# Three big buffers laid out in pairs, with the first transposes split and a new order of work

## The chip, the cores and the metric

The kernel runs on one core of a Trainium2 chip. The metric is the device time of the whole launch in microseconds; three runs of the kernel before gave 157.53 to 160.98, with a median of 159.81.

## The reference

An input `x` of 2048 positions by 512 channels goes through two branches and is mixed by a gate:

```python
g = _sigmoid((x * gate_w).sum(-1, keepdims=True))
a = irfft2(rfft2(x) * (w_r + 1j * w_i), s=(S, D))      # spectral filter over positions and channels
# b: a long convolution over positions, channel by channel:
A = -exp(log_A_real) + 1j * A_imag
C = (C_real + 1j * C_imag) * exp(log_dt)[:, None]
K = 2.0 * einsum("dn,dnl->dl", C, exp((A * dt[:, None])[:, :, None] * pos)).real
b = irfft(rfft(u, 2L) * rfft(K, 2L), 2L)[:, :L] + u * D_skip
return g * a + (1 - g) * b
```

All data are float32.

## The kernel before, in words

All data stay in SBUF, 128 partitions wide. Branch b is a running sum of each channel along the positions when the exponents are small enough; the kernel tests that and otherwise takes a general path, which the inputs of these runs do not take. Branch a is the two-dimensional transform, done as products on TensorE (PE).

The work is cut into steps of one letter and one digit. `PLAN`, a string, lists them, and a loop issues each step's instructions in that order; each engine and each DMA queue then runs its own instructions in the order in which they were issued, waiting for data and for buffers. PSUM is a pool of four buffers of two banks each (tag `ps`), used in rotation. The steps are:

- **C, c**: first half of the transform over the positions. `C` (PE) multiplies a part of the input, lying in `AI`, into a PSUM tile `p_s`; for three parts POOL makes sums and differences `f` first (`F`). `c` (DVE, L259) is one transpose in blocks of 32 by 32 from `p_s` into the buffer `AR`. There are nine parts, seven of 128x1024 and two of 128x512.
- **P, t**: `P` (PE, L372) takes 128 columns of `AR` as the weights, multiplies by a table `s2e` into `p_t`; `t` (ACT, L377) copies out to `et`. There are nine units of this and the following steps; unit 0 is half as large. A product of float32 data appears as two matmul instructions, each with its weight load (PEld).
- **D, d, Z, W, U**: the channel transform (PE, `p_d`, L388), a copy (ACT, L392), sums in PSUM (DVE, L398 to L401) and the multiplication by the filter `w` (DVE, L412 to L416). SP's queue brings `w` for each unit (`l`), and a small row of it (`L`, L363).
- **p, g, h**: sums on POOL (L423, L424 and L435, L436) into `px` and `gt`, and one corrected row (ACT, L442, L443).
- **I, i, V**: the inverse channel transform (PE, `p_v`, L454, weights from `gt`), a copy (ACT, L459), and sums (DVE, L467), which write the buffer `AI`. `K` corrects slot 0 of it.
- **B, b**: inverse transform over the positions, first half, when all units are done: `B` (PE, L486) reads `AI`, four 64x64 tiles of the array at a time, into `p_ia`; `b` (DVE, L489) transposes into `VA`, which is the memory of `AR` under another view. There are eight.
- **Q**: second half (PE, L521): 128x256 of `VA` times a table `s1a` into `p_oa`. `q` (DVE, L542) scales by the gate and adds in one go; `a` (ACT, L532) and `A` (POOL, L536) do the same in two steps. Both end in the stores. There are eight.
- **X, x, y, m, n, r, o, Y, s**: branch b. Load of a 1 MB piece of `XT` (SP, L292), two scalings (ACT, L296 and L300), a running sum (DVE, L304), the even positions (POOL, L308), a DMA that adds the result into `XT` (POOL, L314), the skip term (ACT, L311), transposes of `XT` (PE, `p_y`, L497) and their scaling by one minus the gate into `bs` (ACT, L509).
- **R**: loads of tables; `G`, `J`, `N`: gate, corrections of the filter's edge rows, and the test of the exponents.

Before the change `AR` lies as `[u, t, s]`, with 32 values of `s` together:

```python
    AR = keep.tile([P, 2, P, 32], F32, name="AR")
    VA = AR.rearrange("p u t s -> p (u t) s")
```

so that `P` reads its 128 weights, and `Q` its 256 columns, at steps of 32 floats, and `B` reads `AI` at steps of 256 floats.

Of the kernel before, what the change touches and what calls it, by code (L numbers as in the profile page):

```python
# [9 lines left out]
F32 = mybir.dt.float32  # L10
# [5 lines left out]
P = 128  # L16
# [6 lines left out]
NS = 3  # L23

PLAN = """
C0 X0 c0 C2 c2 F1 F3 C1 C4 c1 c4 C3 c3 R6 C6 N0 N1 F5 C5 c6 c5 C7 c7 R2 N3 R0 R3 C8 c8 x0 P6 y0 X1 t6 J0 R7 J1 R1 P1
l6 R4 m0 y1 x1 m1 J2 t1 D6 d6 P8 t8 P7 l1 n0 N2 l8 t7 D1 L6 d1 n1 Z6 X2 L1 U6 W6 Z1 R5 X3 P0 W1 D8 l0 p6 g6 U1 d8 h6
t0 L8 Z8 L0 G0 o1 l4 l7 W8 o0 L4 U8 D0 d0 L7 D7 d7 G1 p1 I6 l3 o2 o3 Z0 g1 U0 G2 Z7 p8 W0 P4 t4 i6 r0 g8 U7 h1 L3 D4
W7 h8 V6 d4 Z4 W4 y2 p0 U4 P3 t3 x2 I1 o4 I8 i1 x3 r1 m2 y3 i8 V1 G4 R8 g0 l5 G5 G3 L5 o5 p7 P5 h0 p4 V8 o7 n2 m3 o6
D3 d3 g7 l2 t5 P2 D5 h7 I0 Z3 t2 r2 W3 n3 r3 U3 I7 g4 d5 D2 h4 i7 Z5 p3 W5 U5 L2 p5 i0 V0 I4 V7 d2 K0 g3 Z2 i4 U2 h3  # L30
K1 g5 S0 h5 Y2 W2 p2 I3 i3 s2 g2 V4 I5 i5 Y0 V3 h2 s0 V5 Y3 I2 Y1 S1 i2 V2 B7 s3 B3 B4 b7 S3 s1 b3 B2 b4 B5 B6 B1 b2
B0 S2 b5 b6 b1 Y6 s6 Y4 b0 s4 Q6 Q4 a6 a4 Q1 a1 A6 Y7 A4 s7 Y5 Q0 Q2 q0 A1 q2 Q7 q7 s5 Q5 Q3 q5 q3
"""
UNITS = [8, 0, 1, 2, 3, 4, 5, 6, 7]
ORDER = [8, 9, 0, 1, 10, 2, 11, 3, 12, 4, 13, 5, 14, 6, 15, 7, 16]
# [123 lines left out]
def body(ctx: ExitStack, tc: tile.TileContext, x, xg, xt, w, wh, prms, vecs, gw, dskip,  # L159
         c_s1e, c_s1f, c_s2e, c_s2, c_s2v, c_s2r, c_s2q, c_s1b, c_s1a, c_dfw, c_dbw, c_pos, c_eye, out):  # L160
    nc = tc.nc
    V, G, S, T = nc.vector, nc.gpsimd, nc.scalar, nc.tensor
# [3 lines left out]
    def psum(name):  # L166
        return ps.tile([P, 2, 512], F32, tag="ps", name=name)

    keep = ctx.enter_context(tc.tile_pool(name="keep", bufs=1))
    eye = keep.tile([P, P], F32, name="eye")  # L170
    g1 = keep.tile([P, 2, 32], F32, name="g1")
    count = keep.tile([1, 1], I32, name="count")


    AR = keep.tile([P, 2, P, 32], F32, name="AR")
    VA = AR.rearrange("p u t s -> p (u t) s")

    wst = ExitStack()
    work = wst.enter_context(tc.tile_pool(name="work", bufs=1))
# [1 line left out]
    AI = work.tile([P, 17, D], F32, name="AI")  # L181
# [11 lines left out]
    s0, dsk, one, m_, nm = pers[:, 0:4], pers[:, 8:12], pers[:, 12:13], pers[:, 13:14], pers[:, 14:15]  # L193
    s2e = work.tile([P, 17, P], F32, name="s2e")
    s2v = work.tile([P, 64], F32, name="s2v")
# [12 lines left out]
    t_ = {}  # L208

    with tc.manual_schedule():  # L210
# [45 lines left out]
        def c_a(q):  # L256
            k = PARTS[q]
            n = 32 * (k.stop - k.start)
            V.transpose(AR.rearrange("p u (h t) s -> p h u (t s)", h=2)[..., 32 * k.start:32 * k.stop], t_["c", q][:, :, :2 * n].rearrange("p h (u n) -> p h u n", u=2))  # L259


        big, sm = few[:, 1:3], few[:, 3]
# [87 lines left out]
        def nrow(pr):  # L350
            return 64 if pr == 8 else P
# [14 lines left out]
        def P_(u):  # L366
            pr = UNITS[u]
            p = t_["pt", u] = psum("p_t").rearrange("p k (q c r) -> p (k q) c r", q=2, c=2)
            for v in range(nrow(pr) // 64):
                sl, k = (0, 16) if pr == 8 else (2 * pr + v, 2 * pr + v)  # L370
                for q in range(4):
                    T.matmul(p[:, q, :, 64 * v:64 * v + 64], AR[:, q % 2, :, 16 * (q // 2) + sl], s2e[:, k], start=True, stop=True)  # L372

        def t_a(u):
            n = nrow(UNITS[u])
# [86 lines left out]
        def V_(u, ks=(0, 1)):  # L462
            pr = UNITS[u]
            n = nrow(pr) // 64
            ai = AI[:, 2 * pr:2 * pr + n].rearrange("p s (h k t) -> p s h k t", h=2, k=2)
            for k in ks:
                V.tensor_tensor(ai[:, :, :, k], t_["pi", u][:, :n, :, 0], t_["po", u][:, :n], op=ALU.subtract if k else ALU.add)  # L467

# [9 lines left out]

        def B_(k):
            p = t_["pb", k] = psum("p_ia")  # L480
            av = AI.rearrange("p s (e t) -> p t (s e)", e=2)[:, 32 * k:32 * k + 32]
            for x in range(2):
                for z in range(2):
                    r = slice(64 * z, 64 * z + 64)
                    y = 16 * (z ^ x)
                    T.matmul(p[64 * x:64 * x + 64, z], s2v[r], av[r, :, y:y + 16], start=True, stop=True, tile_position=(64 * z, 64 * x))  # L486

        def b_a(k):
            V.transpose(VA[:, 32 * k:32 * k + 32].rearrange("p t (z i) -> p t z i", z=2), t_["pb", k].rearrange("p z (t i) -> p t z i", i=16))  # L489


        def Y_(j):
# [25 lines left out]
        def Q_(j):  # L518
            p = t_["pq", j] = psum("p_oa").rearrange("p k (b d) -> p (k b) d", b=2)
            for k in range(4):  # L520
                T.matmul(p[:, k], s1a[j // 2][:, 4 * j % 8 + k], VA[:, :, 4 * j + k], start=True, stop=True)  # L521

# [16 lines left out]
        def q_a(j):  # L539
# [16 lines left out]

        todo = {
            "f": lambda q: fold(q, V), "F": lambda q: fold(q, G), "C": C_, "c": c_a, "N": lambda k: N_[k](),
            "X": load_x, "x": x_a, "m": scan, "o": skip, "y": y_a, "n": lambda k: even(k, G), "k": lambda k: even(k, V), "r": both, "G": G_, "J": J_, "l": load_w, "L": load_h,
            "P": P_, "t": t_a, "D": D_, "d": d_a, "Z": Z_, "W": lambda u: W_(u, 0, V), "U": lambda u: W_(u, 1, V), "p": p_a, "g": g_a, "h": h_a, "I": I_, "i": i_a, "V": V_,  # L560
            "K": K_, "B": B_, "b": b_a, "Y": Y_, "s": s_a, "S": load_a, "Q": Q_, "q": q_a, "a": a_a, "A": A_a, "R": lambda k: loads[k](),
        }
        for word in PLAN.split():
# [5 lines left out]
    with tc.If(n_small < D):  # L569
        with tc.tile_pool(name="dram", bufs=1, space=bass.MemoryType.DRAM) as dp:  # L570
            Kd = dp.tile([D, L], F32, name="Kd")
            with tc.tile_pool(name="kg", bufs=1) as kg:
# [25 lines left out]
                for c in range(0, D, NC):  # L598
                    def tmp(name, dt=F32):
                        return kg.tile([P, NC, 96], dt, name=name, bufs=2)  # L600

                    pb = pos.rearrange("p (o l) -> p o l", o=1).broadcast_to([P, NC, 96])
# [5 lines left out]
                    for k in range(2):  # L608

                        ri, r, z = tmp("ri", I32), tmp("r"), tmp(f"z{k}")  # L610
# [23 lines left out]
                    for j in range(NC // 4):  # L634
                        for q in range(4):
                            d = NC // 4 * q + j
# [14 lines left out]
            with tc.tile_pool(name="gx", bufs=1) as gx:  # L651
                s1f = gx.tile([P, 2, P], F32, name="s1g")
                nc.sync.dma_start(s1f, c_s1f)
                for dst, isk in ((KR, True), (AG, False)):
# [4 lines left out]
                    for h in range(2):  # L659
# [6 lines left out]
                        for e in range(2):  # L666
                            for c in range(4):
                                o = 32 * c
                                p = psum("p_g1")
                                for u in range(2):  # L670
                                    q = 2 * c + u
# [6 lines left out]
            for i, pr in enumerate(ORDER):  # L678
                rows = 64 if pr == 8 else P
                slots = [2 * pr, 2 * pr + 1] if pr < 8 else ([0] if pr == 8 else [2 * pr - 2, 2 * pr - 1])  # L680
                s2 = gw2.tile([P, 2, 2, 64], F32, name="s2g", bufs=2)
# [16 lines left out]
            p = psum("p_sp")  # L698
# [3 lines left out]
            for c in range(16):  # L702
                p = psum("p_gb")
# [6 lines left out]
            for j in range(8):  # L710
# [7 lines left out]
                for i in range(4):  # L718
                    b = 4 * j + i
                    p = psum("p_go")  # L720
                    for e in range(2):
                        T.matmul(p[64 * e:64 * e + 64, 1, 0:256], gb[:, i], AG[:, b, 256 * e:256 * e + 256], start=True, stop=True)
                    T.matmul(p[:, 0, 0:256], ga[:, i], VA[:, :, b], start=True, stop=True)
                    o = ot[:, i]
# [63 lines left out]
```

## Time and profile before

The profiled execution took 160.45 us, with a span of 158.7 us of recorded work.

| engine | busy, us | share of the span | instructions |
|---|---|---|---|
| PE (matmuls) | 138.0 | 87% | 817 |
| PEld (weight loads) | 100.8 | 64% | 817 |
| DVE | 87.1 | 55% | 127 |
| ACT | 62.2 | 39% | 111 |
| POOL | 70.6 | 44% | 62 |

Weight loads overlap with matmuls. The DMA engines moved 26.56 MB, most of it in the first 40 us. The shares are means over stages with different limits, so they do not say by themselves what an engine's time is worth.

### The profile page before, as it was taken

What the parts mean: (1) busy time and instruction counts of PE and PEld (TensorE: products, weight loads), DVE (VectorE), ACT (ScalarE), POOL (GpSimd) and SP (SyncE); (2) the same over time, 40 slices, a digit from 0 to 9 for tenths busy, and PEclk for the clock granted to TensorE, in tenths of its full rate; (3) what the DMA queues carried; (4) which work ended last, traced back from release to release, by engine and by line L of the source; (5) the groups of instructions that cost most, each with busy time, mean ns of one, the idle gap of its engine ahead of it and who ended that gap; (6) DMA issues with size and microseconds to landing.
All of it is one profiled execution on the core that took longest, in us unless ns stands there. A gap on an engine that the chain in (4) does not pass through costs nothing. (4 is left out here: it accounts for less than half of the span.)

```text
span 158.7 us, 2220 instructions
## 1 busy us (share of the span) xinstructions
PE 138.0 (87%) x817; PEld 100.8 (64%) x817; DVE 87.1 (55%) x127; ACT 62.2 (39%) x111; POOL 70.6 (44%) x62
## 2 busy tenths in 40 slices
PE   7568969999999879959999898779999999999910
PEld 7435659999929758949997687624546447444400
DVE  0117985483599953899479996135664000254440
ACT  0003034813284864599444356850004646500000
POOL 0337011566669963969894999000000067400000
PEclk9999996999999956996899999999999999999995
DMA  4999999889323799723999712000000014174450
GB/s 136 292 319 415 413 393 308 320 302 382 96 82 121 214 203 220 179 52 115 255 213 178 262 28 108 0 0 0 4 0 0 0 46 180 46 266 169 169 192 16
DMA packets 9301, 26.56 MB, mean 167 GB/s; under 512 B 1697, under 2 KB 2497, under 8 KB 8257
## 3 DMA queue, kind: packets, MB, share of 16 engines
q1 hardware_dynamic: 8704, 22.13, 39.4%
q0 software_dynamic: 576, 4.19, 14.0%
q8 instruction: 8, 0.13, 0.3%
q14 instruction: 13, 0.10, 0.2%
HBM read 17.90 MB, written 4.19 MB: 139 GB/s over the span
## 5 line engine op out<-in xcount | busy, mean ns | idle before, releaser
L372 PE MATMUL p_t<-s2e,AR 128*128 128x128 f32 x136 | 31.3, 392 | 3.1 <-DVE AR L259 1.4
L372 PEld LDWEIGHTS p_t<-s2e,AR 128*128 128x128 f32 x136 | 30.6, 312 | 4.1 <-DVE AR L259 1.8
L521 PE MATMUL p_oa<-AR,s1a 128*128 128x256 f32 x64 | 28.0, 609 | 0.0
L521 PEld LDWEIGHTS p_oa<-AR,s1a 128*128 128x128 f32 x64 | 13.0, 205 | 13.6 <-issue 13.4
L388 PE MATMUL p_d<-et,dfw 128*128 128x256 f32 (+1 forms) x72 | 18.7, 411 | 1.2 <-ACT et L377 1.2
L454 PE MATMUL p_v<-dbw,gt 128*128 128x128 f32 x136 | 16.7, 278 | 2.3 <-ACT gt L443 1.2
L454 PEld LDWEIGHTS p_v<-dbw,gt 128*128 128x128 f32 x136 | 15.8, 192 | 3.4 <-ACT gt L443 1.4
L536 POOL TENSOR_TENSOR AI<-AI,qs 128x1024 f32<-128x1024 f32 x2 | 4.8, 2384 | 29.1 <-ACT qs L532 29.1
L486 PE MATMUL p_ia<-AI,s2v 64*64 64x512 f32 x64 | 16.1, 1153 | 1.3 <-ACT bs L509 1.3
L388 PEld LDWEIGHTS p_d<-et,dfw 128*128 128x128 f32 x72 | 14.1, 215 | 4.1 <-ACT et L377 1.4
L542 DVE SCALAR_TENSOR_TENSOR bs<-p_oa,g,bs 128x256 f32<-128x256 f32 x12 | 5.0, 478 | 19.9 <-PE p_oa L521 19.9
L259 DVE STREAM_TRANSPOSE AR<-p_s 128x1024 f32<-128x1024 f32 (+1 forms) x9 | 9.8, 1115 | 10.3 <-PE p_s L254 10.3
L467 DVE TENSOR_TENSOR AI<-p_v,po 128x512 f32<-128x512 f32 (+1 forms) x18 | 10.9, 653 | 6.5 <-ACT po L459 6.5
L423 POOL TENSOR_TENSOR px<-tw 128x512 f32<-128x512 f32 (+1 forms) x9 | 11.3, 1261 | 7.0 <-DVE tw L416 4.4
L489 DVE STREAM_TRANSPOSE AR<-p_ia 128x1024 f32<-128x1024 f32 x8 | 10.0, 1251 | 7.6 <-PE p_ia L486 7.6
L254 PE MATMUL p_s<-AI 64*64 64x256 f32 (+1 forms) x192 | 10.7, 363 | 3.6 <-DMA AI<-in_x_dram 3.6
L377 ACT COPY et<-p_t 128x1024 f32<-128x1024 f32 (+1 forms) x9 | 8.7, 963 | 12.4 <-PE p_t L372 10.7
L308 POOL TENSOR_TENSOR v<-v,uo 128x1024 f32<-128x1024 f32 x4 | 9.6, 2412 | 8.6 <-DVE v L304 8.6
L435 POOL TENSOR_TENSOR gt<-px 128x512 f32<-128x512 f32 (+1 forms) x9 | 11.5, 1277 | 4.3 <-PE p_d L388 4.1
L486 PEld LDWEIGHTS p_ia<-AI,s2v 64*64 64x64 f32 x64 | 6.2, 152 | 9.6 <-issue 7.9
L509 ACT ACTIVATE AI<-p_y,g 128x256 f32<-128x256 f32 x16 | 6.1, 505 | 15.9 <-PE p_y L497 15.9
L254 PEld LDWEIGHTS p_s<-AI 64*64 64x64 f32 x192 | 7.4, 133 | 7.3 <-DMA AI<-in_x_dram 3.1
(67 smaller groups left out, 177.9 us busy)
## 6 DMA issues: line engine op xcount, KB each, us to landing
XT<-in_xt_dram SPq DMA_DIRECT2D x4, 1024.0 KB, 6.0
w<-in_w_dram SPq DMA_DIRECT2D x8, 512.0 KB, 3.8
XT<-v POOLq DMA_DIRECT2D x4, 1024.0 KB, 9.3
AI<-in_x_dram SPq DMA_DIRECT2D x7, 512.0 KB, 8.6
s1a<-in_c_s1a_dram SPq DMA_DIRECT2D x4, 512.0 KB, 4.2
out_dram<-AI SPq DMA_DIRECT2D x8, 256.0 KB, 2.3
out_dram<-bs SPq DMA_DIRECT2D x8, 256.0 KB, 2.7
prm<-in_prms_dram SPq DMA_DIRECT2D x3, 256.0 KB
```

What stands on the lines that cost most here:

```text
L254: T.matmul(p[64 * g:64 * g + 64, h, u * n:u * n + n], s1e[r, 64 * u * i:64 * u * i + 64], xin(q)[r, i, g * n:g * n + n], start=i == 0, sto ...
L259: V.transpose(AR.rearrange("p u (h t) s -> p h u (t s)", h=2)[..., 32 * k.start:32 * k.stop], t_["c", q][:, :, :2 * n].rearrange("p h (u n ...
L308: E.tensor_tensor(v[:, 0:L:2], v[:, 1:L:2], t_["uo", k], op=ALU.subtract)
L372: T.matmul(p[:, q, :, 64 * v:64 * v + 64], AR[:, q % 2, :, 16 * (q // 2) + sl], s2e[:, k], start=True, stop=True)
L388: T.matmul(parts(u)[:, o, 1:3] if h else parts(u)[:, o, 0:4:3], dfw[:, 2 * h + o], t_["et", u][:, 2 * h + o, :, :n], start=True, stop=True)
L423: G.tensor_tensor(po[:, 0], t1[:, :, 0:4:2], t1[:, :, 1:4:2][:, :, ::-1], op=ALU.subtract)
L435: G.tensor_tensor(gv[:, :, 0], src[0], src[1], op=ALU.subtract)
L454: T.matmul(p[:, v, h, o], rows(u, o, v, h), dbw[:, h, o], start=True, stop=True)
L467: V.tensor_tensor(ai[:, :, :, k], t_["pi", u][:, :n, :, 0], t_["po", u][:, :n], op=ALU.subtract if k else ALU.add)
L486: T.matmul(p[64 * x:64 * x + 64, z], s2v[r], av[r, :, y:y + 16], start=True, stop=True, tile_position=(64 * z, 64 * x))
L489: V.transpose(VA[:, 32 * k:32 * k + 32].rearrange("p t (z i) -> p t z i", z=2), t_["pb", k].rearrange("p z (t i) -> p t z i", i=16))
L521: T.matmul(p[:, k], s1a[j // 2][:, 4 * j % 8 + k], VA[:, :, 4 * j + k], start=True, stop=True)
```

## The change

The buffer `AR` becomes `[u, c, t, d]`, where the old `s` is `2c + d`: neighbours in `s` lie in pairs, and a pair's successor in `t` is next to it. `VA`, the other view of the same memory, becomes `[t, b, z]` with pairs `z`. In `AI` the two halves `h` of a channel row become the innermost index. So `P` reads weights at steps of two floats, `Q` reads runs of two floats 64 apart, and `B` reads runs of two floats, over the slots and then over the channels. The writers follow: `c` becomes two transposes of half the size each, whose writes are runs of two floats 256 apart; `b` writes at steps of two floats within 32, and `V` at steps of two floats. The plan has the same 267 steps in another order.

```diff
-C0 X0 c0 C2 c2 F1 F3 C1 C4 c1 c4 C3 c3 R6 C6 N0 N1 F5 C5 c6 c5 C7 c7 R2 N3 R0 R3 C8 c8 x0 P6 y0 X1 t6 J0 R7 J1 R1 P1
+C0 F1 X3 c0 R0 X1 C2 c2 C1 R6 R3 c1 C4 c4 R7 F3 C3 c3 C6 N0 F5 C5 c5 R2 R1 c6 N1 N3 C7 l6 c7 X0 x3 C8 c8 P1 P6 y3 y1
...
-    AR = keep.tile([P, 2, P, 32], F32, name="AR")
-    VA = AR.rearrange("p u t s -> p (u t) s")
+    AR = keep.tile([P, 2, 16, P, 2], F32, name="AR")
+    VA = AR.rearrange("p u c t d -> p (u c t d)").rearrange("p (t b z) -> p t b z", b=32, z=2)
...
         def c_a(q):
...
-            V.transpose(AR.rearrange("p u (h t) s -> p h u (t s)", h=2)[..., 32 * k.start:32 * k.stop], t_["c", q][:, :, :2 * n].rearrange("p h (u n) -> p h u n", u=2))
+            av = AR.rearrange("p u c (h t) d -> p u h t c d", h=2)
+            pv = t_["c", q][:, :, :2 * n].rearrange("p h (u t c d) -> p u h t c d", u=2, c=16, d=2)
+            for u in range(2):
+                V.transpose(av[:, u, :, k], pv[:, u])
...
-                    T.matmul(p[:, q, :, 64 * v:64 * v + 64], AR[:, q % 2, :, 16 * (q // 2) + sl], s2e[:, k], start=True, stop=True)
+                    T.matmul(p[:, q, :, 64 * v:64 * v + 64], AR[:, q % 2, 8 * (q // 2) + sl // 2, :, sl % 2], s2e[:, k], start=True, stop=True)
...
-            ai = AI[:, 2 * pr:2 * pr + n].rearrange("p s (h k t) -> p s h k t", h=2, k=2)
+            ai = AI[:, 2 * pr:2 * pr + n].rearrange("p s (k t h) -> p s h k t", h=2, k=2)
...
-            av = AI.rearrange("p s (e t) -> p t (s e)", e=2)[:, 32 * k:32 * k + 32]
+            av = AI.rearrange("p s (t e) -> p t s e", e=2)[:, 32 * k:32 * k + 32]
...
-                    y = 16 * (z ^ x)
-                    T.matmul(p[64 * x:64 * x + 64, z], s2v[r], av[r, :, y:y + 16], start=True, stop=True, tile_position=(64 * z, 64 * x))
+                    y = 8 * (z ^ x)
+                    T.matmul(p[64 * x:64 * x + 64, z], s2v[r], av[r, :, y:y + 8], start=True, stop=True, tile_position=(64 * z, 64 * x))
...
-            V.transpose(VA[:, 32 * k:32 * k + 32].rearrange("p t (z i) -> p t z i", z=2), t_["pb", k].rearrange("p z (t i) -> p t z i", i=16))
+            V.transpose(VA[:, 16 * k:16 * k + 16].rearrange("p t (y i) z -> p t z y i", y=2), t_["pb", k].rearrange("p y (t z i) -> p t z y i", z=2, i=16))
```

How the order moves is seen best on the engines. Line numbers behind the transposes are three higher in the kernel after. First PE's row from the last product of the input (L254) to the gate (L321, L324); before:

```order
L254 MATMUL p_s_241<-AI 64x256 x16
L372 MATMUL p_t<-s2e,AR 128x2x64 x8
L345 MATMUL p_h<-eye,AI 36x128
L372 MATMUL p_t<-s2e,AR 128x2x64 x8
L388 MATMUL p_d<-et,dfw 128x2x128 x2
L388 MATMUL p_d<-et,dfw 128x256 x2
L372 MATMUL p_t<-s2e,AR 128x2x64 x16
L388 MATMUL p_d<-et,dfw 128x2x128 x2
L388 MATMUL p_d<-et,dfw 128x256 x2
L372 MATMUL p_t<-s2e,AR 128x2x64 x4
```

and now:

```order
L254 MATMUL p_s_258<-AI 64x256 x16
L375 MATMUL p_t<-s2e,AR 128x2x64 x20
L348 MATMUL p_h<-eye,AI 36x128
L391 MATMUL p_d<-et,dfw 128x2x128 x2
L391 MATMUL p_d<-et,dfw 128x256 x2
L391 MATMUL p_d<-et,dfw 128x2x128 x2
L391 MATMUL p_d<-et,dfw 128x256 x2
L324 MATMUL p_gate<-XT,gws 32x512 x16
```

Two and a half units of P (P1, P6, P0) now stand ahead of the first D, and D6 and D1 follow each other; before, P8 and P7 stood between them.

POOL's row from the even passes (L308, L311) of branch b on, before:

```order
L308 TENSOR_TENSOR v<-v,uo 128x1024
L273 TENSOR_TENSOR AI<-AI 128x4
L274 TENSOR_TENSOR AI<-AI 128x4
L275 TENSOR_SCALAR AI<-AI 128x4
L308 TENSOR_TENSOR v<-v,uo 128x1024
L423 TENSOR_TENSOR px<-tw 128x2x2x128
L424 TENSOR_TENSOR px<-tw 128x2x2x128
L435 TENSOR_TENSOR gt<-px 128x2x4x64
L436 TENSOR_TENSOR gt<-px 128x2x4x64
```

and now:

```order
L276 TENSOR_TENSOR AI<-AI 128x4
L277 TENSOR_TENSOR AI<-AI 128x4
L278 TENSOR_SCALAR AI<-AI 128x4
L311 TENSOR_TENSOR v<-v,uo 128x1024 x2
L426 TENSOR_TENSOR px<-tw 128x2x2x128
L427 TENSOR_TENSOR px<-tw 128x2x2x128
L438 TENSOR_TENSOR gt<-px 128x2x4x64
L439 TENSOR_TENSOR gt<-px 128x2x4x64
```

Two of the four even passes stand ahead of the first p (unit 6) in both; they are now those of pieces 3 and 1 of branch b instead of 0 and 1.

SP's queue behind the last part of the input, before:

```order
L292 DMA XT<-in_xt_dram 128x2048
L552 DMA s2e<-in_c_s2e_dram 128x1024
L548 DMA AI<-in_wh_dram 128x72
L546 DMA s2e<-in_c_s2e_dram 128x256
L546 DMA s2e<-in_c_s2e_dram 128x128
L549 DMA eye<-in_c_eye_dram 128x128
L292 DMA XT<-in_xt_dram 128x2048
L553 DMA gws<-in_gate_w_dram 128x128
L553 DMA pers<-in_vecs_dram 128x4
L547 DMA dfw<-in_c_dfw_dram 128x512
L358 DMA w<-in_w_dram 128x1024
L550 DMA dbw<-in_c_dbw_dram 128x768
```

and now:

```order
L295 DMA XT<-in_xt_dram 128x2048
L549 DMA s2e<-in_c_s2e_dram 128x256
L549 DMA s2e<-in_c_s2e_dram 128x128
L295 DMA XT<-in_xt_dram 128x2048
L555 DMA s2e<-in_c_s2e_dram 128x1024
L552 DMA eye<-in_c_eye_dram 128x128
L556 DMA gws<-in_gate_w_dram 128x128
L556 DMA pers<-in_vecs_dram 128x4
L551 DMA AI<-in_wh_dram 128x72
L550 DMA dfw<-in_c_dfw_dram 128x512
L361 DMA w<-in_w_dram 128x1024
L295 DMA XT<-in_xt_dram 128x2048 x2
```

The other two megabytes of `XT` now follow the first `w` directly, ahead of the second and third `w`; before, they came behind all three.

More of the change, by code (lines that the diff above doesn't have):

```diff
@@ L25 @@
 PLAN = """
-C0 X0 c0 C2 c2 F1 F3 C1 C4 c1 c4 C3 c3 R6 C6 N0 N1 F5 C5 c6 c5 C7 c7 R2 N3 R0 R3 C8 c8 x0 P6 y0 X1 t6 J0 R7 J1 R1 P1
[L27 to L32, printed above, removed]
+C0 F1 X3 c0 R0 X1 C2 c2 C1 R6 R3 c1 C4 c4 R7 F3 C3 c3 C6 N0 F5 C5 c5 R2 R1 c6 N1 N3 C7 l6 c7 X0 x3 C8 c8 P1 P6 y3 y1
+m3 t1 P0 x1 X2 t6 J0 J1 J2 L6 t0 l1 m1 N2 D6 n3 d6 R8 n1 D1 Z6 U6 W6 d1 p6 l0 R5 G0 L1 P4 G1 Z1 W1 D0 t4 d0 U1 o7 L0
+g6 D4 l4 Z0 P8 o6 l8 G2 d4 l2 L4 o2 U0 P2 W0 L2 Z4 t8 p1 p0 h6 U4 W4 R4 D8 L8 d8 l5 r3 t2 g1 g0 I6 o3 i6 Z8 y0 p4 G4
+W8 D2 r1 d2 G5 U8 P7 h1 h0 V6 l3 x0 o1 p8 I1 Z2 U2 g4 t7 o0 y2 i1 m0 W2 V1 x2 l7 I0 P3 o4 G3 m2 g8 P5 n0 t3 i0 S3 h4
+D3 o5 L5 V0 d3 L3 p2 Z3 t5 W3 h8 I4 D5 r0 i4 K0 n2 d5 U3 g2 Z5 V4 r2 D7 p3 L7 K1 W5 I8 U5 g3 h2 d7 h3 Z7 p5 I2 S2 I3
+g5 i2 U7 i8 W7 h5 p7 g7 V8 i3 Y2 s2 V2 S1 Y0 I5 i5 V3 Y3 h7 s0 I7 Y1 i7 s3 V5 V7 B5 b5 B3 b3 B6 s1 b6 B4 b4 S0 B1 B0
+B7 b1 b0 B2 b7 Y6 s6 Y7 b2 Y4 s7 s4 Q0 q0 Q4 a4 Q7 q7 Q1 Q6 a1 Q3 A4 Y5 a6 A1 A6 q3 Q2 q2 s5 Q5 q5
 """
```

## The prediction

> **What bounds the kernel now.** I read the windows first, then the chain that ended last, then the engines' timelines. One row for each stretch (busy time and instructions of PE, its weight loads, DVE, ACT, POOL; granted clock; DMA share; GB/s):
>
> ```profile
> 0.00:20.00 20.00, 15.35 (x213) 11.53 (x217) 8.82 (x14) 1.49 (x2) 6.61 (x10) 1.00 0.89 316
> 20.00:40.00 20.00, 18.64 (x107) 17.68 (x100) 11.93 (x14) 9.44 (x10) 8.64 (x10) 0.91 0.92 337
> 60.00:80.00 20.00, 18.04 (x99) 17.03 (x97) 14.26 (x18) 13.85 (x18) 15.89 (x13) 0.85 0.68 164
> 110.00:120.00 10.00, 10.00 (x45) 4.29 (x37) 6.25 (x5) 0.00 (x0) 0.00 (x0) 1.00 0.01 2
> 140.00:150.00 10.00, 10.00 (x24) 4.74 (x23) 4.98 (x12) 0.00 (x0) 0.00 (x0) 1.00 0.54 198
> ...
> 103.92 16.08 PE p_ia L486 x63
> 120.00 2.00 PE p_y L497 x16
> 122.01 10.39 PE p_oa L521 x24
> 132.39 1.79 PE p_y L497 x16
> 134.19 17.33 PE p_oa L521 x40
> ```
>
> There are three stages. Up to about 23 us the input arrives and DMA sets the pace. From 23 to 104 us PE is busy 18 of 20 us, with POOL and DVE at 14 to 16. From 103.92 to 151.5 us PE alone sets the pace, without a gap: the inverse of the sequence transform (B, p_ia) and the last product (Q, p_oa). The last 7.2 us are an eviction and the stores.
>
> Whether that PE time is arithmetic or reading shows in groups of equal size (busy, mean of one):
>
> ```profile
> L372 PE MATMUL p_t<-s2e,AR 128*128 128x128 f32 x136 | 31.3, 392 | 3.1 <-DVE AR L259 1.4
> L372 PEld LDWEIGHTS p_t<-s2e,AR 128*128 128x128 f32 x136 | 30.6, 312 | 4.1 <-DVE AR L259 1.8
> L521 PE MATMUL p_oa<-AR,s1a 128*128 128x256 f32 x64 | 28.0, 609 | 0.0
> L454 PE MATMUL p_v<-dbw,gt 128*128 128x128 f32 x136 | 16.7, 278 | 2.3 <-ACT gt L443 1.2
> L454 PEld LDWEIGHTS p_v<-dbw,gt 128*128 128x128 f32 x136 | 15.8, 192 | 3.4 <-ACT gt L443 1.4
> L486 PE MATMUL p_ia<-AI,s2v 64*64 64x512 f32 x64 | 16.1, 1153 | 1.3 <-ACT bs L509 1.3
> ...
> 16.77 1.07 PE L249 MATMUL p_s<-f,AI 64*64 64x512 f32 x8
> 30.15 1.89 PE L388 MATMUL p_d<-et,dfw 128*128 128x256 f32 x8
> 31.88 7.10 PE L372 MATMUL p_t<-s2e,AR 128*128 128x128 f32 x32
> ```
>
> p_t and p_v have equal shapes and counts, yet p_t takes 31.3/136 = 230 ns apiece and p_v 16.7/136 = 123. The difference is in the weight load (312 against 192): p_t's weights are taken from AR at steps of 32 floats, p_v's lie together. p_oa takes 28.0/64 = 437 ns for 256 columns read at steps of 32 floats; p_d takes (31.88 - 30.15)/8 = 216 for 256 columns in runs. p_ia takes 16.1/64 = 251 with four tiles side by side, at steps of 256 floats; the fold's product of the same shape takes 1.07/8 = 134 from contiguous data. All three are near a factor of two, and all three are what the change re-lays.
>
> One row speaks against stride as the cause: the p_y transposes above also take XT at steps of 32 floats, yet cost 2.00/16 = 125 ns. Each transpose is one instruction, where a product is two, so I take it as another way of reading, and keep some chance for it.
>
> **The change part by part.**
>
> P (L372) reads weights at steps of two floats. Q (L521) reads runs of two, 64 floats apart. B (L486) reads runs of two, one slot or two floats apart. The trace has no PE read of these kinds. One end is no gain, the other the contiguous row: P 136 x (230 - 123) = 14.6 us, Q 64 x (437 - 216) = 14.1 us, B 64 x (251 - 134) = 7.5 us. The nearest rows are other engines' reads at steps of two floats:
>
> ```profile
> L300 ACT ACTIVATE uo<-XT,pers 128x1024 f32<-128x1024 f32 x4 | 5.0, 1248 | 0.0
> L311 ACT ACTIVATE XT<-XT,pers 128x1024 f32<-128x1024 f32 x8 | 8.8, 1142 | 0.0
> L308 POOL TENSOR_TENSOR v<-v,uo 128x1024 f32<-128x1024 f32 x4 | 9.6, 2412 | 8.6 <-DVE v L304 8.6
> L536 POOL TENSOR_TENSOR AI<-AI,qs 128x1024 f32<-128x1024 f32 x2 | 4.8, 2384 | 29.1 <-ACT qs L532 29.1
> ```
>
> ACT pays 9% for every second float (1248 against 1142), POOL 1%. That is far nearer the contiguous end, so I take the contiguous rates.
>
> The Trainium skill, "SBUF — State Buffer" (Specifications), says that memory lines are 16 bytes and that two accesses to each line suffice for full bandwidth. Both new patterns have two, which by that rule gives the same full gains; no run of this case shows it yet.
>
> The first transposes (L259) are split in two, and now write pairs 256 floats apart:
>
> ```profile
> L259 DVE STREAM_TRANSPOSE AR<-p_s 128x1024 f32<-128x1024 f32 x7 | 8.5, 1235 | 5.1 <-PE p_s L254 5.1
> L259 DVE STREAM_TRANSPOSE AR<-p_s 128x512 f32<-128x512 f32 x2 | 1.4, 696 | 5.1 <-PE p_s L254 5.1
> L340 DVE TENSOR_TENSOR AI<-AI 128x18 f32<-128x18 f32 x1 | 0.2, 179 | 0.0
> L341 DVE TENSOR_TENSOR AI<-AI 128x9 f32<-128x9 f32 x1 | 0.2, 168 | 0.0
> L489 DVE STREAM_TRANSPOSE AR<-p_ia 128x1024 f32<-128x1024 f32 x8 | 10.0, 1251 | 7.6 <-PE p_ia L486 7.6
> ```
>
> Half the size costs 696, so a split adds 2 x 696 - 1235 = 157 ns, 1.4 us for nine; between the arrivals that hides, and only the last one's 0.3 us (rounded up) lies on the path. L340 and L341 write to places four floats apart: nine elements more cost 11 ns, 1.2 ns each, DVE's own pace (1235/1024). So I put scattered writes at no cost for these and for L489 and L467; the other end is in the rivals.
>
> The middle, with P short. PE's work there falls from some 73 us (18 of 20 over 81 us) to 58, so the next slowest sets the pace. That is POOL:
>
> ```profile
> 37.12 1.27 POOL L423 TENSOR_TENSOR px<-tw 128x512 f32<-128x512 f32 x1 [2.25 <-DVE tw L416]
> 62.17 0.72 POOL L435 TENSOR_TENSOR gt<-px 128x256 f32<-128x256 f32 x1 [4.10 <-PE p_d L388]
> 86.59 1.26 POOL L423 TENSOR_TENSOR px<-tw 128x512 f32<-128x512 f32 x1 [2.16 <-DVE tw L416]
> 91.53 1.28 POOL L435 TENSOR_TENSOR gt<-px 128x512 f32<-128x512 f32 x1
> 97.85 1.27 POOL L436 TENSOR_TENSOR gt<-px 128x512 f32<-128x512 f32 x1
> ...
> L314 POOL DMA_DIRECT2D XT<-v x4 | 3.8, 940 | 0.3 <-POOL v L308 0.3
> ```
>
> From its first p to its last g it takes 99.1 - 37.1 = 62.0 us. Its work in it: eight units at 91.53 - 86.59 = 4.94 (39.5), the half unit 2.8, two even passes at 2.4 (4.8), four DMA issues (3.6): 50.7. So 11.3 us are waits, behind PE in the end. The new order leaves the same work there (n3 and n1 ahead of p6, n0 and n2 behind). I followed DVE's new row at the old durations: each W or U comes out 1 to 4 us before POOL wants it, also with the four PSUM buffers in rotation (P3 waits for unit 2's multiplications, D7 for unit 3's). I leave 2 us of waits.
>
> The start of that chain hardly moves:
>
> ```profile
> 22.28 1.20 ACT L296 ACTIVATE p_x<-XT,pers 128x1024 f32<-128x1024 f32 x1 [5.30 <-POOL pers L280]
> 26.76 1.01 ACT L377 COPY et<-p_t 128x1024 f32<-128x1024 f32 x1 [2.10 <-PE p_t L372]
> 32.70 0.49 DVE L398 SCALAR_TENSOR_TENSOR p_d<-p_d,pers,ds 128x256 f32<-128x256 f32 x1 [0.34 <-ACT ds L392]
> ```
>
> P1, P6 and P0 now stand ahead of D6 and are short, but ACT's row becomes x3 y3 y1 t1 x1 t6 from 22.3: at 0.9 to 1.2 us each, t6 ends at 28.8. D6 to Z6 took 32.70 - 30.15 = 2.55, Z6 to p6 37.12 - 32.70 = 4.42: p6 at 35.8, 1.3 us earlier. SP's queue brings X3 and X1 forward and X0 and X2 back, all megabytes; by bytes at 316 to 337 GB/s, s2e's second part lands at about 25, just as P6 wants it, and unit 1's w near 34, before its W at 37.
>
> Sum of the middle: 35.8 + 50.7 + 2 = 88.5 for the last g. From there to B it took 103.92 - 99.12 = 4.8 (h, I, i, V, same order at the end): B at 93.3 instead of 103.9.
>
> The tail. B's eight tiles would now take 8 x 1.07 = 8.6 us of PE; DVE's transposes behind them take 8 x 1.25 and become the bound: 1.07 + 10.0 = 11.1 to the first Q, against 122.01 - 103.92 = 18.1. The three Y units, 3 us, fit beneath. Q is 64 x 0.216 = 13.8, with one Y (1.0) between: 14.8, against 29.5. A Q then lasts 1.73 us, and DVE's five evictions (1.66 each), ACT's three (1.57) and four copies of y keep up. The 7.2 us of the end stay; the stores (4.2 MB in about 20 us, 210 GB/s) should fit.
>
> ```profile
> 151.54 1.66 DVE L542 SCALAR_TENSOR_TENSOR bs<-p_oa,g,bs 128x256 f32<-128x256 f32 x4 [1.73 <-PE p_oa L521]
> 125.51 1.57 ACT L532 ACTIVATE qs<-p_oa,g 128x256 f32<-128x256 f32 x4 [1.34 <-PE p_oa L521]
> ```
>
> The clock: between 60 and 80 us, with short idle times, 0.85 was granted; PE will idle more before B, so I add 1.0 us to B. Span: 93.3 + 11.1 + 1.0 + 14.8 + 7.2 = 127.4. The profiled execution took 160.45 for a span of 158.7, 1.75 more: **129 us**, 31 less than its own time. The shown median, 159.81, lies 0.6 below the profiled run; I let 129 stand for the median.
>
> **The rivals.**
>
> *The middle stays as it is.* POOL's 11 us of waits may remain, because the new order ties PE to DVE's release of PSUM. Then only the tail gains: 54.8 to 34.1 us, 160.45 - 20.7 = 140. For it: SP's queue puts two megabytes ahead of unit 1's w. Against: the slack of 1 to 4 us.
>
> *Pairs do not help moving reads.* Then Q and B stay at 437 and 251 ns, the tail at 54.8, and only the middle gains: 93.3 + 54.8 + 1.75 = 150. For it speaks p_y's price; against it, that two other engines read every second float almost for nothing.
>
> *The clock stays low.* The Trainium skill, "TensorE: Matmul & The Clock Gate" (Part 1), says that an idle window halves the clock until a busy one has passed. As a mechanism of this kernel: with PE slack in the middle, B and Q at half rate would cost 17.7 (8 x 2 x 1.03 + 1.25) and 29.5 us, hence 93.3 + 17.7 + 29.5 + 7.2 + 1.75 = 149. Against: 1.00 was granted in each stretch above where PE was busy 10 of 10 us, and from B on it is again busy nearly throughout.
>
> *Slower: DVE pays for the scattered writes.* Sixteen full transposes (seven to nine at the start, eight before Q) lie near the path; the start has some 5 us of slack. If one takes T instead of 1.25 us, the loss is 16 (T - 1.25) - 5. It eats the gain of 31 at T = 3.5; at 5 us (one write to a line in four steps), 129 + 55 = 184. Against: L341's 1.2 ns an element, though nine elements are few.
>
> **How the numbers follow.** Forecast 0.78 (own range 123 to 136), the middle unchanged 0.10, pairs useless for moving reads 0.04, low clock 0.03, slower by DVE 0.04, and 0.01 for several small losses that end within 2% (about what a measurement of this kernel can tell from no change). Faster by over 2%: 0.95; within: 0.01; slower: 0.04. The range takes in the first rival with some room and leaves the rest out: 121 to 143.
>
> **What would show it.** Right: weight loads of p_t near 192 ns and its group near 17 us; p_oa near 14 us; p_ia under 10 us of PE with DVE's transposes back to back behind it; POOL nearly without gaps from 36 to 89 us; first B near 93, first Q near 105. Wrong: transposes well above 1.3 us, p_oa still above 400 ns, or POOL's gaps after p6 summing to more than 6 us.

## The result, and the profile after

The changed kernel takes 132.35 us (median of four, 132.04 to 135.02) against 160.39 of the kernel before beside it (157.53 to 161.1): the ratio is 0.833, with a 95% interval of 0.819 to 0.848. The forecast was 129, with a range of 121 to 143. The profiled execution took 132.04 us for a span of 130.1. Times below are medians, but each trace is of one execution, and the traces of Q undone (149.53 us) and of the early even pass (133.4 us) are of executions slower than the median, so whole times are not read from these two.

The groups that were compared before, now, and the writers of the new layouts (busy us, mean ns of one):

```profile
L375 PE MATMUL p_t<-s2e,AR 128*128 128x128 f32 x136 | 18.0, 289 | 2.8 <-DVE AR L262 1.6
L375 PEld LDWEIGHTS p_t<-s2e,AR 128*128 128x128 f32 x136 | 17.2, 201 | 4.8 <-DVE AR L262 2.3
L457 PE MATMUL p_v<-dbw,gt 128*128 128x128 f32 x136 | 18.1, 291 | 5.2 <-DVE v L307 3.2
L524 PE MATMUL p_oa<-AR,s1a 128*128 128x256 f32 x64 | 14.3, 379 | 0.0
L489 PE MATMUL p_ia<-AI,s2v 64*64 64x512 f32 x64 | 8.4, 604 | 0.1
L262 DVE STREAM_TRANSPOSE AR<-p_s 128x512 f32<-128x512 f32 (+1 forms) x18 | 10.3, 627 | 11.2 <-PE p_s L254 11.2
L470 DVE TENSOR_TENSOR AI<-p_v,po 128x512 f32<-128x512 f32 (+1 forms) x18 | 10.8, 653 | 6.0 <-ACT po L462 6.0
L492 DVE STREAM_TRANSPOSE AR<-p_ia 128x1024 f32<-128x1024 f32 x8 | 9.2, 1216 | 1.3 <-PE p_ia L489 1.3
```

Per instruction, p_t now costs 18.0/136 = 132 ns, the same as p_v; p_oa 223 ns instead of 437; p_ia 131 instead of 251. The writers pay almost nothing: the first transposes, split in two, cost 10.3 us in all, the second 1216 ns each, V's sums 10.8 us (before: 8.5 + 1.4, 1251 ns and 10.9 us).

PE's timeline from B on, and POOL's from its first p to its last g with every wait between them that the trace lists:

```profile
94.07 8.46 PE L489 MATMUL p_ia<-AI,s2v 64*64 64x512 f32 x64
102.46 3.26 PE L500 MATMUL p_y<-eye,XT 128*128 128x128 f32 x24
105.69 10.68 PE L524 MATMUL p_oa<-AR,s1a 128*128 128x256 f32 x48
116.20 1.05 PE L500 MATMUL p_y<-eye,XT 128*128 128x128 f32 x8
117.09 3.63 PE L524 MATMUL p_oa<-AR,s1a 128*128 128x256 f32 x16
...
36.46 1.27 POOL L426 TENSOR_TENSOR px<-tw 128x512 f32<-128x512 f32 x1 [3.33 <-DVE tw L419]
53.94 1.27 POOL L426 TENSOR_TENSOR px<-tw 128x512 f32<-128x512 f32 x1 [0.41 <-DVE count L338]
73.93 1.26 POOL L426 TENSOR_TENSOR px<-tw 128x512 f32<-128x512 f32 x1 [0.97 <-DVE tw L419]
84.27 1.30 POOL L426 TENSOR_TENSOR px<-tw 128x512 f32<-128x512 f32 x1 [0.20 <-DVE tw L419]
88.12 1.26 POOL L439 TENSOR_TENSOR gt<-px 128x512 f32<-128x512 f32 x1
```

POOL's chain lasts 52.9 us instead of 62.0 and waits 1.6 us in it instead of 11. The first B comes at 94.07 instead of 103.92, the last Q ends at 120.72 instead of 151.5.

### The profile page after: what moved, and what is told of

Read it like the earlier page. It is cut to its first block, busy times and chain, and to the rows that moved or that the text cites. A ratio compares the mean times of both kernels' runs of the same rounds, so it can differ in the third digit from the quotient of the medians.

```text
span 130.1 us, 2226 instructions
## 1 busy us (share of the span) xinstructions
PE 107.0 (82%) x817; PEld 85.4 (66%) x817; DVE 85.3 (66%) x136; ACT 62.0 (48%) x111; POOL 70.4 (54%) x62
## 5 line engine op out<-in xcount | busy, mean ns | idle before, releaser
L375 PEld LDWEIGHTS p_t<-s2e,AR 128*128 128x128 f32 x136 | 17.2, 201 | 4.8 <-DVE AR L262 2.3
L375 PE MATMUL p_t<-s2e,AR 128*128 128x128 f32 x136 | 18.0, 289 | 2.8 <-DVE AR L262 1.6
L262 DVE STREAM_TRANSPOSE AR<-p_s 128x512 f32<-128x512 f32 (+1 forms) x18 | 10.3, 627 | 11.2 <-PE p_s L254 11.2
L391 PE MATMUL p_d<-et,dfw 128*128 128x256 f32 (+1 forms) x72 | 16.5, 374 | 0.3 <-ACT et L380 0.2
L470 DVE TENSOR_TENSOR AI<-p_v,po 128x512 f32<-128x512 f32 (+1 forms) x18 | 10.8, 653 | 6.0 <-ACT po L462 6.0
L524 PE MATMUL p_oa<-AR,s1a 128*128 128x256 f32 x64 | 14.3, 379 | 0.0
L254 PE MATMUL p_s<-AI 64*64 64x256 f32 (+1 forms) x192 | 12.3, 403 | 2.2 <-DMA AI<-in_x_dram 2.2
L426 POOL TENSOR_TENSOR px<-tw 128x512 f32<-128x512 f32 (+1 forms) x9 | 11.1, 1237 | 4.9 <-DVE tw L419 4.5
L311 POOL TENSOR_TENSOR v<-v,uo 128x1024 f32<-128x1024 f32 x4 | 10.0, 2490 | 5.3 <-DVE v L307 5.1
L254 PEld LDWEIGHTS p_s<-AI 64*64 64x64 f32 x192 | 8.0, 152 | 6.5 <-DMA AI<-in_x_dram 2.4
L438 POOL TENSOR_TENSOR gt<-px 128x512 f32<-128x512 f32 (+1 forms) x9 | 11.7, 1295 | 0.3
L439 POOL TENSOR_TENSOR gt<-px 128x512 f32<-128x512 f32 (+1 forms) x9 | 11.6, 1287 | 0.0
L500 PE MATMUL p_y<-eye,XT 128*128 128x128 f32 x64 | 9.6, 306 | 2.2 <-issue 2.2
L427 POOL TENSOR_TENSOR px<-tw 128x512 f32<-128x512 f32 (+1 forms) x9 | 11.2, 1240 | 0.0
L419 DVE TENSOR_TENSOR tw<-p_d,w 128x1024 f32<-128x1024 f32 x8 | 9.7, 1216 | 1.8 <-DMA w<-hT 1.7
L500 PEld LDWEIGHTS p_y<-eye,XT 128*128 128x128 f32 x64 | 8.6, 197 | 3.5 <-issue 2.5
```

What stands on the lines that cost most here:

```text
L254: T.matmul(p[64 * g:64 * g + 64, h, u * n:u * n + n], s1e[r, 64 * u * i:64 * u * i + 64], xin(q)[r, i, g * n:g * n + n], start=i == 0, sto ...
L262: V.transpose(av[:, u, :, k], pv[:, u])
L375: T.matmul(p[:, q, :, 64 * v:64 * v + 64], AR[:, q % 2, 8 * (q // 2) + sl // 2, :, sl % 2], s2e[:, k], start=True, stop=True)
L391: T.matmul(parts(u)[:, o, 1:3] if h else parts(u)[:, o, 0:4:3], dfw[:, 2 * h + o], t_["et", u][:, 2 * h + o, :, :n], start=True, stop=True)
L426: G.tensor_tensor(po[:, 0], t1[:, :, 0:4:2], t1[:, :, 1:4:2][:, :, ::-1], op=ALU.subtract)
L427: G.tensor_tensor(po[:, 1, :, ::-1], t2[:, :, 0:4:2], t2[:, :, 1:4:2][:, :, ::-1], op=ALU.add)
```

## The experiments

The three layouts do not depend on each other: `AR` serves P, `VA` (another view of the same memory) serves Q, and `AI` serves B. So each can be undone alone, and the order can be separated from all three.

**The layouts without the order.** The kernel after with the plan of before:

```diff
-C0 F1 X3 c0 R0 X1 C2 c2 C1 R6 R3 c1 C4 c4 R7 F3 C3 c3 C6 N0 F5 C5 c5 R2 R1 c6 N1 N3 C7 l6 c7 X0 x3 C8 c8 P1 P6 y3 y1
+C0 X0 c0 C2 c2 F1 F3 C1 C4 c1 c4 C3 c3 R6 C6 N0 N1 F5 C5 c6 c5 C7 c7 R2 N3 R0 R3 C8 c8 x0 P6 y0 X1 t6 J0 R7 J1 R1 P1
...
```

> All three layouts and the split transposes, with the order of before. If the shorter PE reads are the gain and the order only fits the rest to them: the tail from the first p_ia matmul to the end is as short as with both (36 us instead of 54.8), p_t, p_oa and p_ia cost 18, 14 and 8.4 us of PE, and the middle gets back only part of POOL's waits, since P8 and P7 still stand between D6 and D1: 132 to 138 us. If the order carries the middle's gain, the last g stays near 99 us and the time is 142 to 144.

131.19 us, ratio 0.822 (0.814 to 0.830): all of the gain, a little better than expected and not distinguishable from the kernel after. POOL's first p, its longest later wait and its last g, and PE's last Q:

```profile
35.68 1.27 POOL L426 TENSOR_TENSOR px<-tw 128x512 f32<-128x512 f32 x1 [1.80 <-DVE tw L419]
68.73 2.40 POOL L311 TENSOR_TENSOR v<-v,uo 128x1024 f32<-128x1024 f32 x1 [2.69 <-DMA w<-in_w_dram]
88.41 1.29 POOL L439 TENSOR_TENSOR gt<-px 128x512 f32<-128x512 f32 x1
112.06 8.84 PE L524 MATMUL p_oa<-AR,s1a 128*128 128x256 f32 x40
```

The old order, too, lets POOL run nearly without gaps once P is short (3.0 us of waits after the first p): the last g ends at 89.7 us here and at 89.4 with the new order.

**The order without the layouts.** The kernel before with the plan of after (the whole string exchanged, the other way round).

> The order of after, with all three old layouts and whole transposes. If the reads are the gain: p_t, p_oa and p_ia keep 31, 28 and 16 us of PE, the tail keeps its 54 us, and the order alone saves 0 to 4 us in the middle, since PE bounds it: 156 to 162 us. If the order carries the middle's gain: the last g near 89 us and 149 us.

160.89 us, ratio 1.006 (0.999 to 1.012): nothing. POOL's last g ends at 96.9 instead of 99.1, and the tail, from the first B on, takes 1.3 us of that back (56.1 instead of 54.8 us, with p_ia at 17.4). So the order is not what made the kernel faster, alone or on top of the layouts.

**P undone.** `AR` old, first transposes whole:

```diff
-    AR = keep.tile([P, 2, 16, P, 2], F32, name="AR")
+    AR = keep.tile([P, 2, P, 32], F32, name="AR")
...
-AR[:, q % 2, 8 * (q // 2) + sl // 2, :, sl % 2]
+AR[:, q % 2, :, 16 * (q // 2) + sl]
```

> As after, but AR in the old layout: P reads its weights at steps of 32 floats, the first transposes are whole. If the step sets the price of a weight load: p_t back to 31 us of PE (230 ns each), POOL waits again in the middle, last g 5 to 10 us later, 137 to 142 us. If POOL's chain hides P (PE has slack there): 132 to 134 us though p_t is back at 31. If the price was not the step (p_y reads at such steps for 125 ns): p_t stays near 18 us.

**P at steps of four floats.** One value to 16 bytes:

```diff
-    AR = keep.tile([P, 2, 16, P, 2], F32, name="AR")
+    AR = keep.tile([P, 2, 8, P, 4], F32, name="AR")
...
-AR[:, q % 2, 8 * (q // 2) + sl // 2, :, sl % 2]
+AR[:, q % 2, 4 * (q // 2) + sl // 4, :, sl % 4]
```

> As after, but AR in groups of four: P reads its weights at steps of four floats (16 bytes, one value to a line of 16 bytes), the transposes write runs of four. If two values to a line are what makes the read fast (the Trainium skill, SBUF — State Buffer, Specifications): p_t back to 31 us and the same time as with P undone. If only the distance matters and 16 bytes are near enough: p_t 18 us and 132 us. In between, p_t 24 us, would mean a price that grows with the step.

140.59 us with P undone (ratio 0.881, 0.872 to 0.890) and 142.91 with steps of four (0.898, 0.890 to 0.905). Their p_t groups, first with P undone, then with steps of four:

```profile
L372 PE MATMUL p_t<-s2e,AR 128*128 128x128 f32 x136 | 31.0, 385 | 2.8 <-DVE AR L259 1.4
L372 PEld LDWEIGHTS p_t<-s2e,AR 128*128 128x128 f32 x136 | 30.3, 312 | 4.7 <-ACT gs L324 2.2
```

```profile
L375 PE MATMUL p_t<-s2e,AR 128*128 128x128 f32 x136 | 32.9, 404 | 2.0 <-DMA s2e<-in_c_s2e_dram 1.0
L375 PEld LDWEIGHTS p_t<-s2e,AR 128*128 128x128 f32 x136 | 32.2, 328 | 4.0 <-ACT gs L327 1.9
```

For the weights, four floats apart costs no less than 32 apart (242 and 228 ns apiece); two floats apart costs nearly as little as none (a load of 201 ns, 204 for p_v's in the same trace). So the price does not grow with the distance but has an edge between steps of 8 and 16 bytes. By the rule of the Trainium skill, "SBUF — State Buffer" (Specifications), two accesses to each line of 16 bytes suffice: the runs agree. Steps of four keep the transposes split, so the split is not what made P faster.

**Q undone.** `VA` old, and the write of `b` with it:

```diff
-    VA = AR.rearrange("p u c t d -> p (u c t d)").rearrange("p (t b z) -> p t b z", b=32, z=2)
+    VA = AR.rearrange("p u c t d -> p (u c t d)").rearrange("p (t s) -> p t s", s=32)
```

> As after, but VA in the old layout: Q reads 256 columns at steps of 32 floats, the writes of the second transposes are whole. If runs of two are what makes Q fast: p_oa 28 us of PE (437 ns each) instead of 14.3, all of it in the tail, less some 2 us that the stores now queue at the end: 143 to 147 us. If p_oa stays at 14 us, the runs are not the cause: 132 us.

144.19 us, ratio 0.903 (0.896 to 0.911). The runs of two are the cause of Q's gain, as p_oa is back at 28 us while the second transposes keep their 9.2 us:

```profile
L524 PE MATMUL p_oa<-AR,s1a 128*128 128x256 f32 x64 | 28.1, 611 | 0.0
```

**B undone.** `AI` old:

```diff
-            ai = AI[:, 2 * pr:2 * pr + n].rearrange("p s (k t h) -> p s h k t", h=2, k=2)
+            ai = AI[:, 2 * pr:2 * pr + n].rearrange("p s (h k t) -> p s h k t", h=2, k=2)
...
-            av = AI.rearrange("p s (t e) -> p t s e", e=2)[:, 32 * k:32 * k + 32]
+            av = AI.rearrange("p s (e t) -> p t (s e)", e=2)[:, 32 * k:32 * k + 32]
```

> As after, but AI in the old layout: B reads at steps of 256 floats. If runs of two make B fast: p_ia 16 us of PE instead of 8.4; first Q 18 us behind the first B instead of 11.6, since DVE's transposes no longer bound it: 138 to 140 us. If DVE's writes at steps of two floats (L470) cost anything, that group shrinks from 10.8 us.

141.65 us, ratio 0.888 (0.880 to 0.896), 1.7 us beyond what was expected: from the first B to the first Q it takes 115.21 - 94.53 = 20.7 us, not 18, since p_ia itself costs 17.9 us instead of the 16.1 of before. The new order has a part in that: it lengthens p_ia from 16.1 to 17.4 us with all the old layouts and from 7.3 to 8.4 with the new ones, because B then starts before V's last sums are done. V's sums keep their time, so writing at steps of two floats is free.

```profile
94.53 17.94 PE L489 MATMUL p_ia<-AI,s2v 64*64 64x512 f32 x64
115.21 10.57 PE L524 MATMUL p_oa<-AR,s1a 128*128 128x256 f32 x48
L470 DVE TENSOR_TENSOR AI<-p_v,po 128x512 f32<-128x512 f32 (+1 forms) x18 | 10.8, 651 | 5.7 <-ACT po L462 5.7
```

In shares of the time before, undoing P, Q and B costs 4.8, 7.0 and 5.4%, together 17.2%, and the whole change brings 16.7%. So the three gains add up. Their stages follow each other: with P undone the first B comes 8.6 us later (102.69), and from there to the end it takes 36.4 us, against 36.0 in the kernel after.

**The transposes of y from neighbouring columns.** This tests the row that had spoken against stride. Other columns of `XT` are read, so the skip branch's values are others.

```diff
-                    T.transpose(p[:, k, i], xv[:, i, :, 4 * j + k], eye)
+                    T.transpose(p[:, k, i], XT[:, 2 * i, 128 * (k + 4 * (j % 4)):128 * (k + 4 * (j % 4)) + 128], eye)
```

> As after, but the transposes p_y take 128 neighbouring columns of XT instead of columns 32 floats apart (other values, so the skip branch's part of the output differs). If a transpose reads at steps of 32 floats for nothing: 24 in a row still take 3.0 us (125 ns each). If its reads too pay for the step and 125 ns is the slow price: about 65 ns each, 1.6 us for 24.

133.6 us in one run. The transposes 24 in a row and their weight loads, here and then in the kernel after:

```profile
103.95 3.20 PE L500 MATMUL p_y<-eye,XT 128*128 128x128 f32 x24
L500 PEld LDWEIGHTS p_y<-eye,XT 128*128 128x128 f32 x64 | 8.6, 162 | 3.7 <-issue 2.3 <-DVE AR L492 1.1
```

```profile
L500 PEld LDWEIGHTS p_y<-eye,XT 128*128 128x128 f32 x64 | 8.6, 197 | 3.5 <-issue 2.5 <-DVE AR L492 0.8
```

3.20 us instead of 3.26: no gain, as the first reading expected. But the load itself is shorter. The means of all 64 (162 and 197 ns) mix stretches at different clocks; among the 24 in a row, where 1.00 was granted in both runs, the median load is 141 ns instead of 195. So a transpose's load pays for the step too, 54 ns, which hardly shows in the row of transposes; a product's load rises by 120 ns (192 to 312), and load and matmul together take 107 ns longer (123 to 230).

**Less work for POOL.** If POOL's chain alone bounds the middle, an even pass (2.4 us on POOL) moved to DVE (1.2 us) shortens it:

```diff
-... D3 o5 L5 V0 d3 L3 p2 Z3 t5 W3 h8 I4 D5 r0 i4 K0 n2 d5 U3 g2
+... D3 o5 L5 V0 d3 L3 p2 Z3 t5 W3 h8 I4 D5 r0 i4 K0 k2 d5 U3 g2
```

> As after, but the even pass of piece 2 of branch b is on DVE instead of POOL. If POOL's chain bounds the middle: POOL has 2.4 us less to do, DVE 1.2 more, and the last g, first B and end come 1.5 to 2.4 us earlier: 130 to 131 us. If PE or DVE bound it: no earlier, or up to 1.2 us later.

134.05 us, ratio 0.838 (0.829 to 0.846): no gain. The pass on DVE, and POOL's next DMA, which adds the piece into `XT`:

```profile
74.54 1.22 DVE L311 TENSOR_TENSOR v<-v,uo 128x1024 f32<-128x1024 f32 x1
76.30 0.87 POOL L317 DMA_DIRECT2D XT<-v  x1 [5.83 <-issue]
```

At its place in the plan the pass stood on DVE behind unit 3's work, so POOL stood idle for 5.8 us at the DMA. The trace puts the idle time down to "issue", but the DMA starts 0.5 us after that pass ends. The same pass right behind its running sum (`m2 k2`), where DVE idles:

> As after, with the even pass of piece 2 on DVE, but issued right behind its running sum (m2), where DVE has idle time, so that POOL's DMA of that piece (L317), which waits for it, comes in time. If POOL's chain bounds the middle: POOL's 5.8 us wait at that DMA is gone and the first B comes 1.5 to 2.4 us earlier than after's 94.1: 130 to 130.5 us. If DVE or PE bound it as well: 132 or more.

132.44 us, ratio 0.827 (0.821 to 0.833): no gain that can be told from the kernel after, as the second reading had it. But the traced execution did not bring the pass in time. One step on 32 values (L332), ahead of the running sum on DVE, took 3.25 us instead of the 0.31 in the kernel after, and by the trace POOL's next sum waited 2.94 us for the pass (it reads nothing of it; presumably it takes a buffer that the pass frees):

```profile
63.17 3.25 DVE L332 TENSOR_SCALAR g<-g 128x32 f32<-128x32 f32 x1
68.56 1.23 DVE L311 TENSOR_TENSOR v<-v,uo 128x1024 f32<-128x1024 f32 x1
70.06 1.26 POOL L438 TENSOR_TENSOR gt<-px 128x512 f32<-128x512 f32 x1 [2.94 <-DVE v L311]
```

So taking work from POOL brought nothing in either place, since DVE delivered it late. Whether POOL's chain alone would bound the middle if DVE were in time is not shown.

**The order of the stores.** `A1 A6 q3` becomes `A1 q3 A6`:

> As after, but in the plan q3 stands ahead of A6, so that on SP's queue the stores of q3 no longer wait behind those that POOL's A6 releases. From the last p_oa matmul to the end it took 9.4 us against 7.2 before. If the queue's order is the cause: 1 us of it goes, 131 us. If the write bandwidth is (341 GB/s in the last slices): no change.

133.16 us, ratio 0.833 (0.822 to 0.843): no change, as the second reading expected.

**A small step that blocks.** With the layouts alone, the 32 values of one minus the gate took 4.30 us on DVE; POOL's three sums at that time are shown with it:

```profile
61.00 4.30 DVE L332 TENSOR_SCALAR g<-g 128x32 f32<-128x32 f32 x1
59.92 2.84 POOL L311 TENSOR_TENSOR v<-v,uo 128x1024 f32<-128x1024 f32 x1
62.28 1.70 POOL L438 TENSOR_TENSOR gt<-px 128x512 f32<-128x512 f32 x1
63.52 1.68 POOL L439 TENSOR_TENSOR gt<-px 128x512 f32<-128x512 f32 x1
```

It ends at 65.30, just after the third of them (65.20). It held up DVE's running sum (66.36 to 68.63), and POOL's even pass starts at 68.73. The pass reads that sum, so the 2.69 us of waiting shown above lasted until the sum was done, though the trace names a DMA. The edit, on the layouts with the old order:

```diff
-                V.tensor_scalar(g1[:, 1], g1[:, 0], -1.0, 1.0, op0=ALU.mult, op1=ALU.add)
+                G.tensor_scalar(g1[:, 1], g1[:, 0], -1.0, 1.0, op0=ALU.mult, op1=ALU.add)
```

> Layouts alone (order of before), with the one small step of 32 values for one minus the gate (L332) on POOL instead of DVE. With the layouts alone that step took 4.30 us on DVE, from 61.0 to 65.2, ending with the two POOL sums that ran at the same time; after it the running sum m3 came late and POOL waited 2.7 us. If the step was blocked by POOL's work: it takes 0.3 us on POOL, the wait goes, and the first B comes 2 to 2.7 us earlier: 128 to 129.5 us. If its length was not a wait for POOL: about 4 us on POOL too, and 131 us or more.

128.83 us, ratio 0.807 (0.802 to 0.812), better than the layouts alone and than the kernel after. The step is recorded with 0.68 us on POOL, though POOL's next instruction starts 0.19 us after it, and the first B comes at 92.66 instead of 94.51:

```profile
55.03 0.68 POOL L332 TENSOR_SCALAR g<-g 128x32 f32<-128x32 f32 x1
92.66 7.28 PE L489 MATMUL p_ia<-AI,s2v 64*64 64x512 f32 x64 [1.36 <-ACT bs L512]
```

With `m2 k2` on top of that:

> As the run before, and the even pass of piece 2 on DVE right behind its running sum (m2). If POOL still bounds the middle: another 1 to 2 us earlier, 127 to 128.5 us. If DVE has become the bound there (it is busy 9 of 10 us between 49 and 85 with the layouts alone): no gain, or 1 us later than without.

132.13 us, ratio 0.827 (0.821 to 0.832): 3.3 us lost again. PE's next P, DVE's row ahead of it, and POOL's sum beside the moved pass:

```profile
63.50 3.75 PE L375 MATMUL p_t<-s2e,AR 128*128 128x128 f32 x16 [2.80 <-DVE count L338]
60.34 1.82 DVE L311 TENSOR_TENSOR v<-v,uo 128x1024 f32<-128x1024 f32 x1
63.28 0.14 DVE L338 CAST count<-p_count 1x1 int32<-1x1 f32 x1
61.04 2.26 POOL L438 TENSOR_TENSOR gt<-px 128x512 f32<-128x512 f32 x1
```

The moved pass delays, on DVE's row, the one-value copy out of `p_count` (L338), and the next P waits for it: in the rotation of four buffers it frees the PSUM buffer that P takes, which I infer from the plan. So an even pass on DVE cost more there than it saved on POOL.

## Why the prediction was right, and where it was off

| step | forecast | measured |
|---|---|---|
| P, Q, B per instruction, ns | 123, 216, 134 | 132, 223, 131 |
| first p (unit 6) on POOL, us | 35.8 | 36.46 |
| POOL's waits after it | 2 | 1.6 |
| last g ends | 88.5 | 89.38 |
| first B | 93.3 | 94.07 |
| first Q | 105.4 | 105.69 |
| last Q ends | 120.2 | 120.72 |
| from there to the end | 7.2 | 9.4 |
| span | 127.4 | 130.1 |

- **The rates**: taking every second float as nearly contiguous, by the other engines' rows, held, and undoing each layout alone brought the old price back. P's 132 ns instead of 123 is not a cost of the layout: p_v, whose layout did not change, rose to 133 as well, with a granted clock of 0.91 from 60 to 80 us and 0.83 from 80 to 90. That B's 131 ns came so near to 134 is luck: with the new layouts in the old order it is 7.30/64 = 114, and the rest is the wait for V's last sums. "Pairs do not help moving reads" fell with p_oa at 223 ns and p_ia at 131.
- **The middle**: POOL's chain lasted 52.9 us with 1.6 of waits, so its work was 51.3 us, near the 50.7 worked out. The few waits came out right, but the reason given for them, that DVE had 1 to 4 us of slack, was too generous: at 73.93 and 84.27 POOL waits for DVE's products, and three tries to move work from POOL to DVE gained nothing. The new order, which the sum followed step by step, was not needed: with the old one the last g is only 0.3 us later.
- **B**: the size was right from partly wrong parts, which is luck. DVE's transposes took 9.17 us for eight instead of 10.0, but the first one started 2.4 us after the first B instead of 1.07, as B started while V's last sums (until 95.2) were under way: only two of its 64 matmuls start before they end, and its loads wait 1.0 us for them. The 1.0 us for the clock is not needed: at B 1.00 was granted; it had dropped earlier, between 80 and 90 us (0.83).
- **The end** is the mis-sized term: 9.4 us instead of 7.2, most of the 2.7 us by which the span was longer. SP's last stores, after and then before:

```profile
120.72 2.07 SPq L528 DMA_DIRECT2D out_dram<-bs  x4
122.88 1.83 SPq L528 DMA_DIRECT2D out_dram<-AI  x2
```

```profile
152.45 1.12 SPq L525 DMA_DIRECT2D out_dram<-bs  x2
```

The last issue now ends 4.0 us after the last Q (124.71), before 2.05 (153.57); from it to the end it is 5.4 and 5.1. So the stores do not fit as easily as assumed: the last unit's stores wait on the queue behind those of the unit ahead. It takes both the faster Q and the new order: the end lasts 7.2 us with the old layouts in either order, 7.6 with the new layouts in the old order (120.9 to 128.5), and 9.4 with both. Moving q3's stores ahead of A6's left it at 9.1. Which other part of the new order stretches it was not tried, and that the write bandwidth is the reason is not shown.

- **DVE's writes**: no cost at any of the three places; the rival that would have made the kernel slower had no ground. The split cost 0.4 us in all instead of 1.4.
- **Small slips**: four DMA issues at 0.94 us are 3.8 us, not 3.6; the rival with the low clock takes 1.03 us for a tile where the sum has 1.07; and of the two rows read as writes four floats apart, only L341's are, L340's are two apart. Together they would move the forecast by 0.2 us.

## What to carry to other kernels

When two groups of matmuls of equal shape differ by a factor of two, look at the step in which their operands are read: float32 operands in pairs or two floats apart cost PE almost nothing here, and weights four floats apart as much as 32 (four was not tried for the moving operand). Such a layout can be paid for by the writer, which on DVE was free here. Before reordering a program after such a gain, run the gain with the old order: here the order was worth nothing, and moving a step of 32 values to another engine was worth 2.4 us.

## What the runs showed of the hardware that was not expected

- A DVE instruction on 32 values (L332) took 0.31 us in the kernel after, 1.37 in the kernel before and 4.30 with the layouts alone, and each time it ended within 0.1 us of a POOL instruction. In the longest case it ended only after three POOL instructions in a row. The Trainium skill, "SBUF — State Buffer" (SBUF: two separate sides), says that DVE and GpSimd share a pair of ports under a lock held for a whole instruction, so that the loser waits, but only when DVE's operation runs in a two-port mode or has two inputs in SBUF. The traces agree if L332, which has one input, runs in such a mode, which they do not show; and they add that the wait may last several instructions. POOL can lose as well: a sum of 1.28 us took 2.26 beside an even pass on DVE (1.82 instead of 1.2), which has two inputs in SBUF.
- A transpose's weight load pays 54 ns for a step of 32 floats (141 to 195), a product's 120 ns for as many values (192 to 312). Why they differ stays open.
